# Statistics of one token tile on the scalar engine, and three tiles normed one by one

## The chip, the cores and the metric

The kernel runs on one core of one Trainium2 chip. The metric is the device time of one launch in microseconds. PE is TensorE, DVE is VectorE, ACT is ScalarE, POOL is GpSimd, SP is the engine that issues the DMAs. Ratios are the mean time of one kernel's fast runs over the mean time of the other's fast runs of the same rounds, so not quite the ratio of the medians that stand beside them.

## The reference, cut to what matters

```python
x  = A_x                                     # 2048 tokens x 1024, bf16
xn = layernorm(x)                            # (x - mean) / sqrt(var + 1e-5)
s  = attention(xn, wqkv, wo)                 # 32 heads of 32
y  = layernorm(xn)                           # a second norm, inside the MLP
g  = silu(gelu(y @ w1 + b1) @ w2 + b2)
out = x + s * g
```

The tokens are handled as 16 tiles of 128. Before any matmul can start, a tile has to be loaded, its mean and variance taken, normalised, and transposed.

## The kernel before

The program lists its operations in one order; each engine executes its own part of that list in order, with semaphores between engines. The start ("prologue") goes through the tiles in pairs: normalise, transpose on PE (tiles 0 to 5) or by DMA (tiles 6 to 15), project to K, Q and V, and one unit of attention per pair. From the eighth pair on, attention on ACT and matmuls on PE share the rest of the time.

```python
load_x(0); load_x(1)
load_wq(0, (1,))            # K weights, 512 KB
load_x(2); load_x(3)
load_wq(0, (0,))            # Q weights
load_x(4); load_x(5)
load_wq(0, (2,))            # V weights
... # the other tiles

def stat(tb):               # VectorE: two half statistics, then merge
    for c in range(2): op("vector", bn_stats(...))
    op("vector", bn_aggr(mv[:, tb, :], ...))
def rstd(lo, hi):           # add eps, then power -1/2 on GpSimd
    op("vector" if hi <= 2 else "gpsimd", tensor_scalar(... EPS ...))
    op("gpsimd", tensor_tensor(... mhalf ..., op=pow))
def xnorm(tb):              # VectorE: (x - mean) * rstd
    op("vector", tensor_scalar(xnb[i], x, mv[:, tb, 0:1], lnp[:, 2, tb:tb+1], subtract, mult))

def norm_pair(p):
    lo, hi = 2 * p, 2 * p + 2
    if p == 0:
        stat(0); rstd(0, 1)
        stat(1); rstd(1, 2)
        for t in (0, 1): xnorm(t)
        stat(2); stat(3); rstd(2, 4)
    else:
        if p < NP - 1: stat(hi)
        for t in (lo, lo + 1):
            xnorm(t)
            if t >= TDMA: transp(t)          # DMA transpose
        if p + 1 < NP: stat(hi + 1); rstd(hi, hi + 2)
    if p < 2: ycoef(p)                       # GpSimd: factors of the second norm

# warm-up matmuls around the transposes of tiles 0 and 1
for k, after in ((13, None), (1, 0), (5, 1)):
    op("tensor", warm(k)); ...               # 13, transpose 0, 1, transpose 1, 5

def pro_unit(p):
    if p + 3 < NP: norm_pair(p + 3)
    ...
    pair_kq(p)                               # K and Q projection, 16 matmuls
    for t in (2 * p + 2, 2 * p + 3):
        if t < TDMA: transp(t)
    pair_v(p)
```

The softmax here doesn't subtract the row's maximum and nothing guards it: scores larger than these inputs give would overflow.

## Time and profile before

| | |
|---|---|
| time, median of 3 runs (of 6, with those taken beside the changed kernel) | 1091.45 us (1091.34) |
| span of the profiled run | 1088.8 us |
| busy: PE, ACT, DVE | 99%, 96%, 58% of the span |
| first K/Q projection starts | 10.32 us |
| first scores start | 15.90 us |
| projection of tiles 8 and 9 starts (the "hand-over") | 31.37 us |

The last three rows are the marks. Up to the hand-over PE has gaps; after it PE has next to none, so the hand-over says how long the prologue took. The prediction below shows the chain up to it.

One part of the trace is needed that the prediction does not show: PE around the first tiles (timeline of PE, kernel before; columns: start us, duration us, engine, line, operation and tiles, count, idle time before and what ended it).

```profile
8.50 0.62 PE L380 MATMUL ps<-ident,hT 128*128 128x128 bf16 x8 [0.16 <-DVE hT L353]
8.95 1.24 PE L733 MATMUL ps<-ident 128*128 128x512 bf16 x5
10.32 1.91 PE L681 MATMUL ps<-xnT,wq 128*128 128x256 bf16 x16
```

These are tile 1's eight transposes, five warm-up matmuls that do no work but keep PE busy, and the first projection. Eight transposes in 0.62 us and five warm-ups in 1.24 are PE's fast pace.

### The profile page before, as it was taken

What the parts mean: (1) busy time and instruction counts of PE and PEld (TensorE: products, weight loads), DVE (VectorE), ACT (ScalarE), POOL (GpSimd) and SP (SyncE); (2) the same over time, 40 slices, a digit from 0 to 9 for tenths busy, and PEclk for the clock granted to TensorE, in tenths of its full rate; (3) what the DMA queues carried; (4) which work ended last, traced back from release to release, by engine and by line L of the source; (5) the groups of instructions that cost most, each with busy time, mean ns of one, the idle gap of its engine ahead of it and who ended that gap; (6) DMA issues with size and microseconds to landing.
All of it is one profiled execution on the core that took longest, in us unless ns stands there. A gap on an engine that the chain in (4) does not pass through costs nothing.

```text
span 1088.8 us, 61814 instructions
## 1 busy us (share of the span) xinstructions
PE 1077.2 (99%) x29156; PEld 701.0 (64%) x29156; DVE 628.4 (58%) x1399; ACT 1041.1 (96%) x1192; POOL 21.7 (2%) x66
## 2 busy tenths in 40 slices
PE   8999999999999999999999999999999999999998
PEld 5766666666666666666666666666666666666665
DVE  8388742477732576642377743378733377635556
ACT  6799998999999999999999999999999999999993
POOL 3400000000000000000000000000000000000000
PEclk9999999999999999999999999999999999999999
DMA  7844356323374223445333264423264333674434
GB/s 246 162 142 135 118 157 164 113 68 110 101 171 120 59 71 107 121 104 146 87 105 99 69 158 120 126 81 110 81 130 120 89 115 110 196 207 105 108 92 124
DMA packets 209336, 131.92 MB, mean 121 GB/s; under 512 B 52538, under 2 KB 200250, under 8 KB 209082
## 3 DMA queue, kind: packets, MB, share of 16 engines
q1 hardware_dynamic: 209082, 127.97, 43.1%
q8 instruction: 228, 3.74, 1.5%
q14 instruction: 26, 0.21, 0.1%
HBM read 104.87 MB, written 12.06 MB: 107 GB/s over the span
## 4 chain that ended last, share of the span: by engine, by line
PE 55%; ACT 42%; DVE 2%; DMA 1%; issue 0%; POOL 0%
ACT P L856 38%; PE ps L389 34%; PE ps L844 9%; PE ps L873 6%; PE ps L876 6%; ACT u L559 4%; DVE stats L325 1%; PE ps L681 1%; PE ps L697 1%; DMA xnT<-hT 1%; DVE hT L353 0%; DMA OT<-in_A_x_dram 0%; ACT thz L603 0%; DVE mv L327 0%; DVE wq L663 0%
## 5 line engine op out<-in xcount | busy, mean ns | idle before, releaser
L856 ACT ACTIVATE P<-ps 128x1024 bf16<-128x1024 f32 x1024 | 968.8, 1085 | 8.7 <-PE ps L844 4.0
L873 PE MATMUL ps<-P,VP 128*32 128x256 bf16 x4096 | 256.5, 273 | 0.0
L876 PE MATMUL ps<-P,ones 128*32 128x256 bf16 x4096 | 256.4, 273 | 0.0
L389 PE MATMUL ps<-hT,war 128*32 128x352 bf16 (+1 forms) x5376 | 225.4, 309 | 0.0
L389 PE MATMUL ps<-yTc,war 128*32 128x352 bf16 (+1 forms) x5376 | 225.3, 309 | 0.0
L844 PE MATMUL ps<-QT,KT 32*128 32x256 bf16 x4096 | 203.4, 273 | 2.8 <-ACT P L856 0.2
L389 PEld LDWEIGHTS ps<-hT,war 128*32 128x32 bf16 x5376 | 127.9, 96 | 74.2 <-issue 25.4
L389 PEld LDWEIGHTS ps<-yTc,war 128*32 128x32 bf16 x5376 | 127.4, 96 | 74.2 <-DVE xb L542 19.0
L844 PEld LDWEIGHTS ps<-QT,KT 32*128 32x128 bf16 x4096 | 60.7, 92 | 114.9 <-issue 60.4
L599 DVE TENSOR_SCALAR zh<-ps,b2h 128x352 f32<-128x352 f32 (+1 forms) x48 | 27.4, 572 | 182.9 <-PE ps L389 182.9
L565 DVE SCALAR_TENSOR_TENSOR hT<-u,xb 128x352 bf16<-128x352 f32 (+1 forms) x168 | 84.4, 509 | 68.4 <-ACT u L559 68.4
L542 DVE TENSOR_SCALAR xb<-ps,b1T 128x352 f32<-128x352 f32 (+1 forms) x168 | 96.2, 572 | 47.8 <-PE ps L389 43.2
L873 PEld LDWEIGHTS ps<-P,VP 128*32 128x32 bf16 x4096 | 109.2, 97 | 20.3 <-issue 1.3
L876 PEld LDWEIGHTS ps<-P,ones 128*32 128x32 bf16 x4096 | 109.4, 97 | 18.7
L389 PE MATMUL ps<-xnT,wq 128*32 128x352 bf16 (+1 forms) x2688 | 112.7, 309 | 0.0
L389 PEld LDWEIGHTS ps<-xnT,wq 128*32 128x32 bf16 x2688 | 63.8, 96 | 37.2 <-DVE xb L542 9.1
L552 DVE SCALAR_TENSOR_TENSOR u<-u,xb 128x352 f32<-128x352 f32 (+1 forms) x168 | 82.4, 508 | 1.9
L548 DVE TENSOR_TENSOR u<-xb 128x352 f32<-128x352 f32 (+1 forms) x168 | 82.4, 507 | 0.7
L559 ACT ACTIVATE u<-u 128x704 f32<-128x704 f32 (+1 forms) x84 | 71.9, 860 | 0.0
L389 PE MATMUL ps<-xnT,OT 128*32 128x352 bf16 (+2 forms) x1568 | 62.9, 306 | 0.2 <-DVE wq L663 0.2
L389 PE MATMUL ps<-wq,xnT 128*32 128x256 bf16 x1536 | 50.8, 274 | 0.0
L389 PEld LDWEIGHTS ps<-xnT,OT 128*32 128x32 bf16 x1568 | 37.9, 96 | 19.7 <-DVE wq L663 7.7
(53 smaller groups left out, 474.6 us busy)
## 6 DMA issues: line engine op xcount, KB each, us to landing
war<-in_B_w_dram SPq DMA_DIRECT2D x336, 256.0 KB, 3.3
wq<-in_A_wqkv_dram SPq DMA_DIRECT2D x36, 128.0 KB, 2.4
OT<-in_A_x_dram SPq DMA_DIRECT2D x16, 256.0 KB, 5.7
xnT<-in_A_x_dram SPq DMA_DIRECT2D x16, 256.0 KB, 3.2
out_dram<-wq SPq DMA_DIRECT2D x15, 256.0 KB, 2.1
y_scratch<-OT SPq DMA_DIRECT2D x14, 256.0 KB, 2.5
gT_scratch<-gst SPq DMA_DIRECT2D x32, 88.0 KB, 3.1
xnT<-in_A_wo_dram SPq DMA_DIRECT2D x8, 256.0 KB, 4.1
```

The source lines that it names most:

```text
L325: op("vector", lambda e, c=c: e.bn_stats(stats[:, tb, c, :], xt[:, c * 512:(c + 1) * 512]), r=[("xst", tb)], w=[("st", tb, c)], c=677.0)
L389: ins = e.matmul(outs(j), lhsT=lhs(j), rhs=rhs, start=start, stop=stop, tile_position=(0, 32 * j), skip_group_check=True)
L542: x0 = op("vector", lambda e: e.tensor_scalar(xb[:, 0:n], bank(bk, 0, n), b1T[:, f:f + 1], None, op0=ALU.add), r=[("b", bk), "b1"], w=[kx] ...
L548: x = op("vector", lambda e: e.tensor_tensor(ub[:, 0:n], xb[:, 0:n], xb[:, 0:n], op=ALU.mult), r=[kx], w=[ku], c=151 + 1.042 * n)
L552: x = op("vector", lambda e: e.scalar_tensor_tensor(ub[:, 0:n], ub[:, 0:n], 1.0 / 0.044715, xb[:, 0:n], op0=ALU.add, op1=ALU.mult), r=[kx, ...
L559: x = op("scalar", lambda e: e.activation(ut[:, :, 0:n], ut[:, :, 0:n], ACT.Tanh, scale=0.7978845608028654 * 0.044715), r=kus, w=kus, c=48 ...
L565: op("vector", lambda e: e.scalar_tensor_tensor(hT[:, fq, 0:n], ut[:, i, 0:n], 1.0, xq[:, 0:n], op0=ALU.add, op1=ALU.mult), r=[kus[i], kq] ...
L599: x0 = op("vector", lambda e: e.tensor_scalar(zh[:, 0:n], bank(bk, 0, n), 0.25, b2h[:, nb:nb + 1], op0=ALU.mult, op1=ALU.add), r=[("b", bk ...
L844: ins = e.matmul(bank(bks[j], kh * 256, (kh + 1) * 256), lhsT=KT[i2][32 * j:32 * j + 32, k0:k0 + 128], rhs=QT[i2][32 * j:32 * j + 32, qb * ...
L856: op("scalar", lambda e, p=p, sl=sl: e.activation(pb[:, 2 * p:2 * p + 2, :, :].rearrange("p a b q -> p (a b q)"), ps[:, sl * 1024:(sl + 1) ...
L873: e.matmul(bankq(ACC, j, 0, QW), lhsT=VP[vp][:, kb, vo + 32 * j:vo + 32 * j + 32], rhs=pb[:, j, kh, :], start=first, stop=False, tile_posi ...
L876: ins = e.matmul(bankq(ACC, j, QW, 2 * QW), lhsT=ones[:, 0:32], rhs=pb[:, j, kh, :], start=False, stop=last, tile_position=(0, 32 * j), sk ...
```

## The change

The intent: VectorE is the chain of the prologue, ScalarE is idle there. So tile 1's statistics go to ScalarE as two passes with a sum (of x, then of the squared difference), VectorE is free for other tiles, and tiles 1 to 3 are normalised as soon as each can be.

```diff
+        def stat_scalar(tb):
+            op("scalar", activation(xnb[8], xt, Identity, scale=-1.0 / D, accum_out=neg))
+            op("scalar", activation(xnb[8], xt, Square, bias=neg, accum_out=sq))
+            op("scalar", activation(mean, neg, Copy, scale=-1.0))
+            op("gpsimd", tensor_scalar(..., sq, 1.0 / D, EPS, mult, add))
+            op("gpsimd", tensor_tensor(... pow))
+            op("gpsimd", tensor_scalar(mv[:, tb, 1:2], sq, 1.0 / D, ...))   # variance
...
             if p == 0:
                 stat(0)
                 rstd(0, 1)
-                stat(1)
-                rstd(1, 2)
-                for t in (0, 1):
-                    xnorm(t)
-                stat(2)
+                stat_scalar(1)
+                xnorm(0)
+                bn_half(2, 0)
+                xnorm(1)
+                bn_half(2, 1)
+                bn_merge(2)
+                rstd(2, 3)
                 stat(3)
-                rstd(2, 4)
+                xnorm(2)
+                rstd(3, 4)
+            elif p == 1:
+                stat(4)
+                xnorm(3)
+                stat(5)
+                rstd(4, 6)
             else:
```

(Arguments are cut. `bn_half` and `bn_merge` are the two parts of the old `stat`.)

## The prediction

> **What bounds the kernel now.** I read the page first, then the chain of waits in order of time for the first 60 us, then the timeline of each engine there, the DMA issues one at a time, and windows around the one stall I found. The page says where not to look:
>
> ```profile
> PE 1077.2 (99%) x29156; PEld 701.0 (64%) x29156; DVE 628.4 (58%) x1399; ACT 1041.1 (96%) x1192; POOL 21.7 (2%) x66
> L325 DVE BATCH_NORM_STATS2 stats<-OT 128x6 f32<-128x512 bf16 x32 | 20.1, 671 | 2.3 <-DMA OT<-in_A_x_dram 2.3
> ```
>
> From about 49 us on, TensorE and ScalarE alternate as the bound and VectorE has room. All that the change touches (the statistics of tiles 0 to 3) lies in the first 15 us. So it can only move the start of the steady stretch, and a shift there moves the end by the same amount: everything after it is driven by PE and ACT. In the chain of waits of the start these lines carry it (start, duration, what):
>
> ```profile
> 5.36 1.20 DVE stats L325 x2
> 7.07 0.80 POOL lnp L334
> 8.44 1.21 DVE stats L325 x2
> 23.77 0.87 DVE hT L353 x2
> 24.64 0.85 DVE stats L325 x2
> 25.49 5.84 DMA xnT<-hT
> 31.37 1.92 PE ps L681 x16
> ```
>
> The reader is to see that the chain of the start is VectorE, nearly unbroken from 3.6 to 25.5 us, then one DMA transpose of tile 9 that takes 5.84 us, then TensorE for good. The timeline gives TensorE's own slack at that hand-over:
>
> ```profile
> 31.37 1.92 PE L681 MATMUL ps<-xnT,wq 128*128 128x256 bf16 x16 [0.57 <-DMA xnT<-hT]
> ```
>
> TensorE was ready 0.57 us earlier, at 30.80. So two chains race to the projection of tiles 8 and 9: **A**, VectorE then the DMA, ends at 31.37; **B**, the PE/ACT chain of the first four pairs, at 30.80. The time moves by how far the later of the two moves. Behind it TensorE has no further gap: the next transposes land 2 us or more before they are needed.
>
> Why that transpose took 5.84 us when those of tiles 6 to 8 took 2.7 to 2.8 shows in the windows (columns: PE, PEld, DVE, ACT, POOL busy, clock, DMA share, GB/s):
>
> ```profile
> 27.00:28.00 1.00, 1.00 (x11) 0.90 (x10) 0.96 (x4) 1.00 (x2) 0.17 (x1) 1.00 3.18 95
> 28.00:29.00 1.00, 1.00 (x12) 0.88 (x11) 1.00 (x3) 1.00 (x2) 0.00 (x0) 1.00 0.03 3
> q8 instruction: 1, 0.02, 2.5%
> ```
>
> In 27 to 29 us one 16 KB packet of an instruction queue arrives (the last line is the DMA view of 27 to 29.5) and the transposes stand still. The page has 228 such packets, 3.74 MB: at 64 bytes each, an estimate with the size that the skill gives (below), that is 58,000 instructions, which is TensorE's 29,156 matmuls and 29,156 weight loads. So I read it as TensorE's own program being fetched; it moves with chain B.
>
> **What the Trainium skill says.** "ScalarE: Activation LUTs", What ACT_TABLE_LOAD costs: an ACTIVATE takes 186 ns + 0.833 N, and 93 ns more for each pointer operand. For N = 1024 with two pointers that is 1225 ns; the trace has 1250 (the three y tiles, scale and bias from a tile), so it agrees. The same page, Table sets: cheap functions are in every set, and a function outside the active set costs another load of about 2.7 us. The trace has one load, 1283 ns, at 0.72 us. "Perfetto Trace Analysis", Per-instruction lifecycle: instructions are 64 bytes, and the DVE and ACT have a wait queue where an instruction waits for its semaphores before it goes to the execution FIFO; I take from it that a waiting instruction holds up all that stand behind it. The trace agrees: VectorE sits 2.28 us before the first statistics although later work is queued. No page that I read prices the accumulator output of an ACTIVATE.
>
> **The change, part by part.**
>
> *Removed from VectorE:* the statistics of tile 1, from 5.36 to 6.83 in the chain (1.47), and its add of eps, 0.17: 1.64 us.
>
> *Added to ScalarE,* idle until 8.16 now: two passes over 1024 elements and a copy of one column. Each pass with one pointer is 1250 less 93, some 1.16 us; the copy some 0.19 (the two bias copies). Tile 1 was issued at 1.18 and took 3.1, so it landed at 4.25. First pass to 5.4, second to 6.65, if the accumulator is free. Then GpSimd: add 0.22, power 0.56 to 0.79, so tile 1's factor is there at about 7.75 (now at 7.87). The copy ends at 6.9, before ScalarE is wanted by the first transpose (7.3).
>
> *Moved on VectorE:* tile 0's normalisation, now at 6.90, goes as soon as its power ends (5.45 + 0.56), at 6.05. Then comes half of tile 2's statistics, **ahead of** tile 1's normalisation. That is the step that decides. Tile 2's load:
>
> ```profile
> 2.11 0.58 SPq L274 DMA_DIRECT2D OT<-in_A_x_dram  x1
> OT<-in_A_x_dram SPq DMA_DIRECT2D x1, 256.0 KB, 6.0
> 8.36 1.28 DVE L325 BATCH_NORM_STATS2 stats<-OT 128x6 f32<-128x512 bf16 x2
> ```
>
> Issued at 2.11 and landed 6.0 later: 8.11. Before, VectorE reached tile 2 at 8.36 and never saw that wait. After, it is ready for tile 2 at 6.6 and must stand until 8.1, with tile 1's normalisation (ready at 7.75) behind it. The 1.64 us removed are thus turned into a wait of 1.5 us.
>
> From 8.13 on, with steps between starts from the timeline (half statistics 0.60, whole tile 1.43, one normalisation 0.47, the split merge about 0.1 more): half of tile 2 at 8.13; normalise 1 at 8.73, to 9.27; second half 9.20; merge 9.9; statistics of 3 at 10.0 to 11.5; normalise 2 at 11.46; statistics of 4 at 11.9; normalise 3 at 13.36, to 13.9; statistics of 5 at 13.8; those of 6 at 15.26. Before, tile 6 began at 14.90. So **chain A comes 0.36 us later**: the part from tile 2 on has one normalisation more in it (0.47) and the split (0.1), and begins 0.23 earlier. The powers of tiles 2 and 3 (done at 11.2 and 12.7) are no bound in this order, nor are the coefficients on GpSimd, 2.64 us that end near 15.3.
>
> *Chain B:* tile 1 normalised at 9.27 instead of 8.44; transpose (0.62) to 9.95; evacuation 1.04 to 11.03, instead of 10.18; first K/Q projection at 11.15 instead of 10.32, done at 13.06. Tile 2 is then ready and its transpose no longer waits (0.92 now), tile 3's goes at 13.95, V at 14.5 instead of 14.2. The first scores come at 16.2 instead of 15.90: **B some 0.3 later**, at 31.1.
>
> Both chains, and with B the instruction fetch, shift nearly rigidly by 0.3 to 0.36 us. Sum: 1091.45 + 0.35 = 1091.8.
>
> **The rivals.** *R1, no wait for tile 2.* If its load lands near 6.5 in most runs, VectorE keeps its gain: tile 1 at 7.75, and from there to the statistics of tile 6 some 6.4 us instead of the present 7.01, so A is 0.7 to 0.75 earlier and B, through tile 3, about 0.8. Time 1090.8. For it: a load's landing depends on what else moves. Against: tile 2 stands behind tile 1 and 512 KB of weights, and the wait is a full 1.5 us.
> *R2, the fetch misses the transpose.* If tile 9's transpose ends before the fetch, or the fetch goes elsewhere, it takes 2.8 us as tile 8's does, and the bubble of 0.57 goes; B at 31.1 then sets the end, 0.27 earlier than now: 1091.2. Against: both shift together.
> *R3, ScalarE becomes the bound.* A second table load of 1.28 plus what goes with it, or a dear accumulator, brings tile 1's factor to about 9.2 instead of 7.75, past 8.73: 0.5 later still, 1092.3. Against: the square is listed by the skill as a cheap function, and there is one microsecond of room.
> *R4, other orders later.* The program places VectorE's and ScalarE's small tasks by its own clock; a shift may reorder a few and cost or give some tenths anywhere.
>
> **Range and chances.** I give the wait (0.35 later) a little over half, R1 a quarter, R2 an eighth, R3 less; weighted, the expectation lies near 1091.5. Runs of before spread over 1090.32 to 1091.67. I name 1091.6, from 1090.2 to 1092.8. Two per cent is 22 us, more than the whole stretch touched, so both outer chances are half a per cent each.
>
> **What would show it.** In the changed profile: VectorE idle of about 1.5 us before the first statistics after tile 0's normalisation, ended by the load of x; two ACT passes of 1.1 to 1.3 us from 4.3; one table load; tile 1's normalisation at 8.7; the first projection near 11.15; the projection of tiles 8 and 9 at 31.6 to 31.8 after a transpose that still takes over 5 us. I am wrong if tile 1 is normalised before 8 us, if that last transpose lands in under 3.5, or if the steady stretch reaches the end by another length than now (1088.8 less 31.4).

## The result, and the profile after

| | before | after |
|---|---|---|
| median of 6 runs | 1091.34 us (1090.32 to 1093.14) | 1091.07 us (1089.82 to 1093.17) |
| ratio, 95% interval | | 0.9998 (0.9985 to 1.0011): the same |
| span of the profiled run | 1088.8 us | 1089.4 us |
| tile 1 normalised | 7.89 us | 8.75 us |
| first K/Q projection | 10.32 us | 12.27 us |
| first scores | 15.90 us | 17.14 us |
| hand-over | 31.37 us | 31.97 us |

The traced run is 0.6 us longer in its span, and the hand-over accounts for all of it: from there to the end it is 1057.4 us after and 1057.5 before. In the median of the runs even that does not show. The timeline of VectorE in the changed kernel:

```profile
5.82 0.55 DVE L359 TENSOR_SCALAR hT<-OT,mv,lnp 128x1024 bf16<-128x1024 bf16 x1 [0.68 <-POOL lnp L340]
8.14 0.69 DVE L324 BATCH_NORM_STATS2 stats<-OT 128x6 f32<-128x512 bf16 x1 [1.78 <-DMA OT<-in_A_x_dram]
8.75 0.53 DVE L359 TENSOR_SCALAR hT<-OT,mv,lnp 128x1024 bf16<-128x1024 bf16 x1
15.14 1.23 DVE L324 BATCH_NORM_STATS2 stats<-OT 128x6 f32<-128x512 bf16 x2
```

Tile 0 is normalised a microsecond earlier than before (5.82 for 6.90). Then VectorE stands for 1.78 us, and the bracket says for what: the load of x, here tile 2's, which lands at 8.12. Only after half of that tile's statistics comes tile 1's normalisation. The last line, tile 6's statistics, comes 0.24 us after the old 14.90.

ScalarE's timeline shows that tile 1 was not short of its statistics:

```profile
4.25 1.06 ACT L713 ACTIVATE hT<-OT 128x1024 bf16<-128x1024 bf16 x1 [2.25 <-DMA OT<-in_A_x_dram]
5.22 0.19 ACT L713 ACTIVATION_READ_ACCUMULATOR hT<-OT 128x1 f32 x1
5.44 1.15 ACT L714 ACTIVATE hT<-OT,mneg 128x1024 bf16<-128x1024 bf16 x1
6.49 0.19 ACT L714 ACTIVATION_READ_ACCUMULATOR hT<-OT,mneg 128x1 f32 x1
6.58 0.19 ACT L715 ACTIVATE mv<-mneg 128x1 f32<-128x1 f32 x1
...
10.38 1.02 ACT L389 ACTIVATE xnT<-ps 128x1024 bf16<-128x1024 bf16 x1 [2.25 <-PE ps L386]
```

The two passes took 1.06 and 1.15 us, each sum was fetched by an instruction of its own (0.19), and GpSimd had tile 1's factor at 7.61, 1.14 us before VectorE came to use it. The last line is ScalarE copying tile 1's transposes to `xnT`, where the projection reads them; it is done at 11.40.

PE's timeline answers to the one shown of before:

```profile
9.34 1.00 PE L386 MATMUL ps<-ident,hT 128*128 128x128 bf16 x8 [2.06 <-DVE hT L359]
10.14 2.34 PE L758 MATMUL ps<-ident 128*128 128x512 bf16 x5
12.27 2.19 PE L687 MATMUL ps<-xnT,wq 128*128 128x256 bf16 x16
```

PE had idled 2.06 us for tile 1, and then the same eight transposes took 1.00 us instead of 0.62 and the same five warm-ups 2.34 instead of 1.24. PE had fallen to half its pace, and it reached the projection 1.95 us later than before, not 0.83 as the prediction had it. The 1.12 between them are some 0.3 from the slow transposes and some 0.8 from the slow warm-ups: tile 1 was in place at 11.40, but PE was still at its warm-ups.

The chain of waits of the changed kernel no longer names a DMA transpose at the hand-over. Its chain (start, duration, what):

```profile
2.11 6.01 DMA OT<-in_A_x_dram
...
8.75 0.54 DVE hT L359
...
9.34 1.00 PE ps L386 x8
10.34 2.13 PE ps L758 x5
12.48 1.98 PE ps L687 x16
...
32.04 1.85 PE ps L687 x16
```

From tile 2's load through tile 1's normalisation, the slow transposes and the warm-ups, then PE without a break to the hand-over. (The chain counts a piece of PE from the end of the one before, so its 32.04 is the hand-over at 31.97.) And the transpose of tile 9 (DMA view at its issue; the last column is us to landing), which had taken 5.8 before:

```profile
xnT<-hT SPq DMA_TRANSPOSE x1, 2.8
```

Apart from these, the two programs run the same instructions in the same order: PE and the DMA queue from end to end, ACT and VectorE outside the prologue.

### The profile page after: what moved, and what is told of

Its sections match the earlier page's. It is cut to its first block, busy times and chain, and to the rows that moved or that the text cites. A ratio compares the mean times of both kernels' runs of the same rounds, so it can differ in the third digit from the quotient of the medians.

```text
span 1089.4 us, 61820 instructions
## 1 busy us (share of the span) xinstructions
PE 1078.9 (99%) x29156; PEld 702.0 (64%) x29156; DVE 627.3 (58%) x1395; ACT 1043.4 (96%) x1197; POOL 23.0 (2%) x70
## 4 chain that ended last, share of the span: by engine, by line
PE 56%; ACT 42%; DMA 1%; DVE 0%; issue 0%; SPq 0%
ACT P L881 38%; PE ps L395 33%; PE ps L869 9%; PE ps L898 6%; PE ps L901 6%; ACT u L565 4%; PE ps L687 1%; PE ps L703 1%; DMA OT<-in_A_x_dram 1%; ACT thz L609 0%; PE ps L386 0%; PE ps L758 0%; DVE wq L669 0%; DVE zh L605 0%; DVE wq L671 0%
```

## The experiments

All kernels below gave correct results. The times cannot carry the argument: the reference spread over some 2 us, and the effect looked for is about 1. So each kernel is judged by the marks of its trace, and the times are given for what they are worth. After the first comparison, the calls ran on three chips (5, 6 and 7). The theory after the first comparison: **(1)** VectorE meets tile 2's load and holds up tile 1; **(2)** while it waits PE idles and loses its fast pace, which costs as much again. The rivals: the wait is harmless and the warm-ups or the new work are in the way; or VectorE's amount of work decides, not its waits.

All marks in one table (us; "tile 2" is the landing of its load; the last column is the median with that of the kernel before from the same call):

| kernel | tile 2 | tile 1 normed | first projection | first scores | hand-over | span | median (before) |
|---|---|---|---|---|---|---|---|
| before | 8.11 | 7.89 | 10.32 | 15.90 | 31.37 | 1088.8 | 1091.34 |
| before, again | 7.96 | 7.63 | 10.06 | 15.63 | 31.08 | 1088.7 | 1092.15 (1091.21) |
| changed | 8.12 | 8.75 | 12.27 | 17.14 | 31.97 | 1089.4 | 1091.07 (1091.34) |
| changed, again | 8.07 | 8.70 | 11.03 | 16.09 | 30.92 | 1088.7 | 1090.51 (1091.21) |
| tile 1 first | 7.16 | 8.38 | 10.72 | 16.38 | 31.21 | 1090.2 | 1091.65 (1090.38) |
| changed, early load | 6.32 | 7.51 | 9.85 | 14.97 | 29.81 | 1087.4 | 1089.31 (1090.38) |
| the same, again | 5.80 | 7.50 | 9.84 | 15.15 | 29.99 | 1088.0 | 1090.36 (1091.21) |
| before, early load | 5.92 | 7.87 | 10.30 | 15.91 | 31.31 | 1090.5 | 1091.85 (1091.21) |
| changed, late load | 10.21 | 10.85 | 14.40 | 19.16 | 33.99 | 1091.7 | 1093.95 (1090.63) |
| changed, PE kept busy | 8.39 | 9.02 | 11.35 | 16.41 | 31.24 | 1089.2 | 1090.78 (1090.38) |
| changed, one warm-up | 7.33 | 7.97 | 10.29 | 15.35 | 30.18 | 1089.3 | 1091.06 (1090.38) |
| before, cold start | 7.54 | 7.69 | 11.40 | 15.99 | 30.82 | 1088.8 | 1091.20 (1090.63) |
| ScalarE part alone | 8.28 | 7.56 | 9.90 | 15.85 | 30.69 | 1089.0 | 1090.49 (1090.63) |
| one-by-one part alone | 7.19 | 7.54 | 9.97 | 15.54 | 31.00 | 1089.9 | 1090.79 (1090.63) |

### Take the wait away: tile 2 loaded before the first weights

```diff
-        load_wq(0, (1,))
         load_x(2)
+        load_wq(0, (1,))
         load_x(3)
```

> The changed kernel, with tile 2's load issued before the first weights instead of after them; nothing else. Theory: tile 2 lands near 5 us instead of 8.12, the 1.78 us wait of VectorE is gone (at most 0.9 remains, for tile 1's factor from GpSimd), tile 1 is normalised at 7.65, tile 6's statistics begin near 14.2 instead of 15.14, first projection near 10.1, first scores near 15.1, projection of tiles 8 and 9 near 30.0. The whole 0.6 to 0.7 us that the change was to bring shows, span near 1087.5. Rival (the first weights become the bound in place of the tile): they land near 8.1 and are not wanted before 10, so nothing is lost; if they land after 10.2 the first projection waits for them and the gain is gone.

VectorE's timeline in this kernel:

```profile
5.86 0.55 DVE L359 TENSOR_SCALAR hT<-OT,mv,lnp 128x1024 bf16<-128x1024 bf16 x1 [0.68 <-POOL lnp L340]
6.34 0.69 DVE L324 BATCH_NORM_STATS2 stats<-OT 128x6 f32<-128x512 bf16 x1
7.51 0.55 DVE L359 TENSOR_SCALAR hT<-OT,mv,lnp 128x1024 bf16<-128x1024 bf16 x1 [0.47 <-POOL lnp L717]
```

The wait of 1.78 us is gone; what is left is 0.47 for tile 1's own factor. Every mark came where expected except the landing itself (6.32, not 5): first projection 9.85, first scores 14.97, hand-over 29.81, 1.56 us before that of the kernel before in its first trace and 1.27 before its second. The weights landed at 7.83 and nothing waited for them. The median was 1.07 below that of the kernel before, ratio 0.9995 (0.9982 to 1.0007), so unresolved by times. A second draw:

> The changed kernel with tile 2's load issued before the first weights, a second draw on this chip: first projection near 9.9, first scores near 15.0, projection of tiles 8 and 9 at 29.8 to 30.0, that is 1.0 to 1.5 us before the kernel before; median 0.5 to 1.5 us below its reference. If the first draw was luck of the landing, first scores come at 15.9 or later.

First projection 9.84, scores 15.15, hand-over 29.99; median 0.85 below the reference, ratio 0.9995 (0.9981 to 1.0008). Both draws agree in the trace.

### Is the early load worth something by itself?

The same edit on the kernel before.

> The kernel before, with tile 2's load issued before the first weights. Theory (only the changed order of VectorE meets that load): nothing moves, since VectorE reaches tile 2 at 8.36 with or without it; first projection 10.3, first scores 15.9, projection of tiles 8 and 9 at 30.8 to 31.4, time same. Rival (the earlier load is worth something by itself, and the changed kernel with the early load gains from that alone): first scores come 0.5 us or more earlier here too, span near 1087.5.

Tile 2 landed at 5.92 and nothing moved: first projection 10.30, scores 15.91, hand-over 31.31. The kernel before never waited for that load. Chip 7 has all four combinations; the hand-over came at 31.08 with neither, 31.31 with the early load alone, 30.92 with the change alone and 29.99 with both (first scores 15.63, 15.91, 16.09 and 15.15). So the early load pays only with the change, and the change shows its full gain only when that load is early.

### Make the wait longer

Tile 2's load goes behind the second weights (`load_x(3); load_wq(0, (0,)); load_x(2)`).

> The changed kernel with the suspected wait made longer: tile 2's load issued behind the second weights, to land near 10.3 instead of 8.1. Theory: VectorE idles some 3.9 us after tile 0 instead of 1.78, tile 1 is normalised at 10.9, TensorE idles over 4 us and runs tile 1's transposes and the warm-ups at the slow pace; first projection at 13.9 to 14.6, first scores at 18.6 to 19.4, projection of tiles 8 and 9 at 33.4 to 34.2, about 2.0 to 2.5 us behind the first trace of the changed kernel, time up by 0.2 per cent. Rival (tile 2's landing is not on the path): first projection and scores as in the changed kernel, at 11.0 to 12.3 and 16.1 to 17.1.

VectorE's and PE's timelines:

```profile
10.23 0.69 DVE L324 BATCH_NORM_STATS2 stats<-OT 128x6 f32<-128x512 bf16 x1 [3.84 <-DMA OT<-in_A_x_dram]
11.43 1.04 PE L386 MATMUL ps<-ident,hT 128*128 128x128 bf16 x8 [4.15 <-DVE hT L359]
12.26 2.34 PE L758 MATMUL ps<-ident 128*128 128x512 bf16 x5
```

All marks fell into the expected ranges: the load 2.09 later than in the changed kernel, tile 1 2.10 later, the first projection 2.13, the hand-over 2.02. Here the times resolve it: ratio 1.0032 (1.0018 to 1.0045), 3.3 us in the median. (That is slower by more than the hand-over's 2.6 over the old 31.37; the rest, below 1 us, is of the size by which the stretch after the hand-over varies.) The load of tile 2 is on the path, and one for one.

### Keep PE busy through the wait

Ten warm-up matmuls instead of one between the transposes of tiles 0 and 1: `(13, None), (10, 0), (5, 1)`.

> The changed kernel with ten warm-up matmuls instead of one between the transposes of tile 0 and of tile 1; order on VectorE unchanged. Theory (what makes TensorE late beyond the wait is its clock): the gap of 2.06 us is filled, tile 1's transposes from 9.34 take 0.6 instead of 1.0, the five warm-ups 1.2 instead of 2.3, first projection near 11.15 instead of 12.27 and first scores near 16.0 instead of 17.14; span 0.6 to 1.1 shorter than the changed kernel's 1089.4 unless the DMA transpose of tile 9 now meets the fetch, when it is that which ends last, near 31.6. Rival (the clock plays no part): first projection stays at 12.27 or comes later by what the nine cost.

```profile
6.93 2.32 PE L758 MATMUL ps<-ident 128*128 128x512 bf16 x10
9.61 0.62 PE L386 MATMUL ps<-ident,hT 128*128 128x128 bf16 x8 [0.35 <-DVE hT L359]
10.07 1.24 PE L758 MATMUL ps<-ident 128*128 128x512 bf16 x5
```

Tile 2 landed 0.27 later than in the changed kernel's first trace and tile 1 was normalised 0.27 later, and yet the first projection started 0.92 earlier: the transposes took 0.62 and the warm-ups 1.24. That is the pace. It does not prove that the ten warm-ups kept it: the unaltered kernel kept it too, in its second trace (below). The hand-over came at 31.24.

### Fewer warm-ups after tile 1

`(13, None), (1, 0), (1, 1)`.

> The changed kernel with one warm-up matmul instead of five after tile 1's transposes. Rival theory (the warm-ups themselves stand in the way of the first projection): it starts at 11.5 instead of 12.27 and runs at its usual 1.9 us, first scores 0.8 earlier, near 16.4. Theory of the clock: it starts at 11.5 but its sixteen matmuls go at 0.21 us instead of 0.11 for a microsecond or more, so it ends at 14.2 to 15 as the changed kernel's does at 14.46, and the first scores come within 0.5 of 17.14; span within 0.5 of 1089.4.

Inconclusive for the slow pace. Tile 2 happened to land at 7.33, so tile 1 was normalised at 7.97, and PE stayed fast: tile 1's transposes took their 0.06 us each. At the fast pace the warm-ups cost nothing: from tile 1's normalisation to the first projection it is 2.32 us here with one warm-up, and 2.33 in the second trace of the changed kernel with five. What fewer warm-ups would save at the slow pace stays untested; the 0.8 us above is what the first trace suggests.

### The slow pace by itself

The kernel before with one warm-up instead of thirteen at the start.

> The kernel before with one warm-up matmul at the start instead of thirteen: what the slow pace of TensorE costs by itself, with VectorE's order untouched. Tile 0's transposes 0.11 us apart instead of 0.06, tile 1's as well, the five warm-ups 0.43 apart: first projection at 11.4 to 11.9 instead of 10.32, its sixteen matmuls partly at 0.21; first scores at 16.9 to 17.6 instead of 15.90, projection of tiles 8 and 9 at 31.9 to 32.5 instead of 31.4. If the pace plays no part, first projection stays at 10.3 and first scores at 15.9.

A miss, and a useful one. PE was slow as intended (tile 0's and tile 1's transposes 0.11 us apart, the warm-ups 0.43), and the first projection started at 11.40, as expected. But the first scores came at 15.99, not 16.9 to 17.6, and the hand-over at 30.82, not 31.9 to 32.5. In the old order PE waits 0.92 us for tile 2's normalisation after that projection anyway, so most of a slow start is absorbed there. In the changed kernel tile 2 is normalised early and that slack is gone.

### The changed order on VectorE, put right

`xnorm(1)` moved ahead of `bn_half(2, 0)`.

> The changed kernel, with tile 1's normalisation moved ahead of the first half of tile 2's statistics on VectorE. Theory (the wait for tile 2's load holds up tile 1, TensorE idles over 2 us and its clock falls): tile 1 is normalised at 7.65 us instead of 8.75, its transposes and the five warm-up matmuls run at the fast pace (0.06 and 0.22 us apart, not 0.11 and 0.43), the first projection starts near 10.1 instead of 12.27, the first scores near 15.1 instead of 17.14, the projection of tiles 8 and 9 at 30.0 if its DMA transpose meets no instruction fetch and near 31 if it does. Span 1087.5 to 1088.5 in the profile, by 0.1 per cent or less faster than before. Rival (the wait is harmless, TensorE was late for another reason such as its own instructions or the five warm-ups): the first projection stays after 11.5.

Missed, for a reason outside the edit: in this execution tile 1's load landed at 4.97 instead of 4.0 to 4.3, and tile 2's at 7.16. Tile 1's factor was late and it was normalised at 8.38. So this trace does not test the order. The nearest test is the ScalarE part alone (below), where tile 1 also goes ahead of tile 2's statistics: tile 2 landed at 8.28, and tile 1 was normalised at 7.56. This trace shows one thing for (2): PE idled some 1.9 us here too and kept its fast pace (transposes 0.055 us apart).

### One part at a time

The ScalarE statistics with the old pairs:

> One part alone: statistics of tile 1 on ScalarE, but the tiles normed as pairs in the old order (tile 1 ahead of tile 2's statistics, tiles 2 and 3 together after those of tile 4). Theory: VectorE meets no new wait that holds up tile 1, which is normalised near 7.6 (8.3 if its own load lands late, at 5), but it reaches tile 2 at 8.1 at the earliest, and there its load decides: tile 6's statistics begin 0.2 to 0.3 before the old 14.90, first projection near 10.0, first scores near 15.6, a gain of 0.2 to 0.3. So the 1.64 us taken from VectorE are worth the 0.25 between 8.36 and the landing of tile 2. Rival (VectorE's work is what counts): first scores 0.7 or more earlier, by 15.2.

VectorE waited 1.10 us for tile 1's factor, normalised that tile at 7.56, then waited 0.20 for tile 2 until 8.30 (its landing was 8.28 here), and tile 6's statistics began at 14.85 instead of 14.90. First scores 15.85, where 15.6 was expected. The 1.64 us taken from VectorE became waits, here more for the factor than for the load; the rival (its amount of work decides) falls. For tile 6's statistics 14.6 to 14.7 was expected; the landing was 0.2 later than assumed.

One by one, with the statistics left on VectorE:

> The other part alone: statistics of tile 1 stay on VectorE, tiles 2 and 3 are normed one by one. Theory: tile 1 is normalised at 7.89 and TensorE stays at the fast pace, tile 2 is normalised at 11.2 instead of 12.58 but tile 3 at 13.1 instead of 13.01, and V and the first scores wait for tile 3: first scores 15.9 to 16.1, tile 6's statistics at 14.9 to 15.0, time same. Rival (norming one by one is where the gain lies): first scores by 15.5.

First scores at 15.54, which at face value is the rival's figure. But the first tile landed 0.35 earlier in this trace (3.27 against 3.62) and all that follows starts from it: tile 1 was normalised 0.35 earlier too. Less that shift, 15.89. The "before, again" trace, with its first tile at 3.36, has 15.63. So no gain.

### Both kernels again

> The changed kernel unaltered, a second draw. The first traces show tile 2's load landing anywhere from 7.2 to 8.4 us for the same issue order, so the wait and the clock of TensorE are a matter of the execution. Theory (the change is worth what the load leaves of it): the first projection starts between 10.1 and 12.5 and follows tile 1's normalisation, which starts when tile 2's load has landed plus 0.6; projection of tiles 8 and 9 between 30.0 and 32.2. Median within 1 us of the kernel before. Rival (the 12.27 us of the first trace are the rule): first projection again at 12.1 to 12.5.

> The kernel before unaltered, against itself: what the method can tell. Median within 0.8 us of its own reference. In the trace the first projection stays near 10.3 whenever tile 2 lands before 8.36, as VectorE does not reach it earlier; projection of tiles 8 and 9 at 30.8, or later if its DMA transpose is held up, as in the first trace (31.37).

PE in the changed kernel's second trace:

```profile
9.29 0.62 PE L386 MATMUL ps<-ident,hT 128*128 128x128 bf16 x8 [1.93 <-DVE hT L359]
9.75 1.24 PE L758 MATMUL ps<-ident 128*128 128x512 bf16 x5
11.03 1.92 PE L687 MATMUL ps<-xnT,wq 128*128 128x256 bf16 x16
```

The wait for tile 2 is nearly the same (it landed at 8.07, tile 1 was normalised at 8.70), but PE kept its pace through an idle time of 1.93 us. So (1) came in both draws and (2) is a matter of the execution: the first projection differs by 1.24 us where tile 1's normalisation differs by 0.05. What decides it fits the page "TensorE: Matmul & The Clock Gate", Part 1: the clock is set by activity in free-running windows of 3413 ns. The traces record the granted clock. In the first trace it is full from 6.00, half from 9.41 and full from 12.83, steps of 3.41 and 3.42 us; with the late load full from 4.50, half from 11.32 (two such steps) and full from 14.74; in the second trace full from 5.21 on. How busy PE was in these windows (columns: window, length, PE busy and matmuls, clock, DMA share, GB/s; first trace, second trace, late load):

```profile
6.00:9.41 3.41, 1.35 (x14) 1.00 1.06 352
9.41:12.83 3.42, 3.42 (x16) 0.50 1.10 379
5.21:8.62 3.41, 1.86 (x14) 1.00 1.00 316
7.91:11.32 3.41, 0.00 (x0) 1.00 1.07 367
11.32:14.74 3.42, 3.31 (x15) 0.50 1.08 398
```

After a window with 1.35 us of PE work, or with none, the clock was halved; after one with 1.86 us it was not, nor after the least busy window of the other traces, 1.67 us (the kernel before with the early load, 4.21 to 7.62). A fixed length of gap does not fit: PE's last work before the fall ended at 7.29 in both of these traces, and the clock fell 2.1 us after it in the first and 4.0 us after it with the late load. No run here set the phase on purpose.

The kernel before, against itself, came out at 1.0008 (0.9995 to 1.0020), its median 0.94 above its own reference where at most 0.8 was expected. That is what the times can tell.

## Why the prediction was right or wrong

The time was 1091.07 where 1091.6 was named, inside the range. That says little: the median of the kernel before was 1091.34, and it came out 0.94 above itself in another call, so a range of 2.6 us would have held almost any effect of this size. The trace has the hand-over 0.6 us later where the working had 0.35, and two of its steps failed on the way, the pace of PE and the transpose of tile 9; that the sum came near is partly luck. By its own steps:

- **What is removed and where the bound lies: right.** The shift at the hand-over reached the end: in the first two traces the rest after it agrees within 0.1 us. Over all fourteen it was 1057.4 to 1059.2, so a single span can hide a shift of this size.
- **ScalarE's part: right, one term missing.** Passes of 1.06 and 1.15 where 1.16 each was said (the first has no pointer operand); reading each sum costs 0.19 us, not foreseen. There was one table load, at 0.72, so rival R3 did not come; nor did R4, as the later orders are the same. Tile 1's factor was there at 7.61 for 7.75.
- **The wait for tile 2, "the step that decides": right.** 1.78 us for 1.5 said; it is larger because tile 0 was normalised at 5.82, not 6.05, its load having landed at 3.40. Tile 1 at 8.75 for 8.73. That a waiting instruction holds up those behind it is shown here, by tile 1, ready at 7.61; the 2.28 us that the prediction gave for it show less, as all that was queued then needed tiles that had not landed either.
- **Chain A "0.36 us later": right in size up to the DMA.** Tile 6's statistics at 15.14 for 15.26, so 0.24. The 0.12 between them is in the steps, 7.00 us from tile 2 to tile 6 instead of 7.13. Against the second trace of the kernel before (14.63, its first tile having landed 0.26 earlier) the changed kernel is 0.5 later: the old start followed tile 0's landing, the new one follows tile 2's.
- **Chain B "some 0.3 later": the term that failed.** The working carried tile 1's transposes at 0.62 us and left out the five warm-ups, because in the trace of before they are hidden behind the evacuation. With PE slow, the transposes took 1.00 and the warm-ups 2.34, and the first projection came at 12.27, not 11.15. The first scores were 1.24 later instead of 0.3. When PE stays fast (second trace), the working holds: 11.03 and 16.09 for 11.15 and 16.2.
- **"Both chains, and with B the instruction fetch, shift nearly rigidly": wrong.** Tile 9's transpose took 2.8 us in the first trace, which the prediction had named as a sign of being wrong, and 5.2 in the second, and in neither did PE wait for it. With tile 1's statistics on VectorE and a fast PE it landed at 30.95 to 31.33 in all four traces and was what PE waited for; in none of the other ten was it. So rival R2 came to pass in its mechanism in the first trace, where B alone, slowed, set the hand-over, and only in its effect in the second. There it gave back about what chain A lost: the hand-over was at 30.92 against 31.08 for the kernel before on the same chip, although the first scores were 0.46 later.
- **R1, the gain without the wait: undersized.** Its step on VectorE held (6.46 us from tile 1's normalisation to tile 6's statistics in the first draw with the early load, for 6.4). It put the time some 0.65 earlier. With the early load the hand-over came 1.1 to 1.6 earlier than in the two traces of the kernel before, because the transpose of tile 9 (landing at 28.88 and 29.45) no longer ended the wait either.

What stays open: why tile 9's transpose is held up by different amounts. A 16 KB instruction packet falls into its time in each of the traces where it took 4 us or more, but in the changed kernel's first trace one started at 28.22 too, half a microsecond before the landing, and did no harm; so it was with the late load. That the packet is the cause was only argued. The DMA records speak against the simplest form of it: in seven traces single packets of the transpose, which otherwise take some 0.02 us, stood for 2.1 to 2.4, and they had started 0.2 to 0.5 us before the instruction packet did.

The version with tile 2 loaded early is the best one found by the trace: spans of 1087.4 and 1088.0 against 1088.8 and 1088.7. The times point the same way by 0.85 and 1.07 us in the median, but with intervals that include no difference.

## What to carry to other kernels

Before work is moved off an in-order engine, look up when the data of the next instruction in its queue lands: work removed ahead of a load that lands no earlier for it turns into a wait, and that wait holds up everything behind it, here a tile that was ready a microsecond earlier. Gaps that this makes on TensorE can cost twice, as it may come out of them at half pace (in the first trace 0.83 us of wait and 1.12 of slow pace). And where an effect is a thousandth of the time and runs differ by two thousandths, mark a point in the trace that everything must pass, and compare that.

## What the Trainium skill lacked or had wrong

- "ScalarE: Activation LUTs" says that an ACTIVATE can give an accumulator output, but gives no cost. Here each one brought an ACTIVATION_READ_ACCUMULATOR of 0.19 us. Its formula held: 1.06 us measured against 1.04 for immediate operands, 1.15 against 1.13 with one pointer.
- "TensorE: Matmul & The Clock Gate" advises no idle gaps over about 3 us. Here a gap of 2.06 us was enough in one execution (eight transposes in 1.00 instead of 0.62 us), while 1.93 us was not in another. The page's free-running windows account for it only in part: its table has the clock fall after an idle window, and here the window of the fall held 1.35 us of PE work, while 1.67 kept the clock. How little counts as idle the page does not say.
- "DMA: Bandwidth & Descriptors" has nothing that we found on how much a queued load's landing differs between executions: tile 2's, always fourth in the same queue, landed between 7.2 and 8.4 us in the ten traces with the old load order.
- The same page prices DMA transposes, but not what they meet: tile 9's took 2.8 to 5.8 us from issue to landing in these traces, with an instruction packet of 16 KB falling into the long ones (and into the last half microsecond of the two short ones).
- No page that we read says how far a steady stretch of the same instructions varies. Here it took 1057.4 to 1059.2 us. Part of that falls near 960 us, where in the trace with the longest such stretch (the kernel before with the early load) PE stands 0.87 us for no reason that the profile shows, while the DMA moves some 340 GB/s:

```profile
959.98 0.59 PE L389 MATMUL ps<-hT,war 128*32 128x320 bf16 x11 [0.87 <-issue]
```
